# Banded attention and a two-layer MLP on one core: the second layer's 512-token blocks as Strassen's seven products

## The chip, the cores and the metric

The kernel runs on one core of a Trainium2 chip. The core has five engines, each with its own instruction queue: TensorE (PE in the profile; its weight loads are shown apart as PEld), VectorE (DVE), ScalarE (ACT), GpSimd (POOL) and SyncE (SP), which here only issues DMAs. TensorE writes its results to PSUM, eight banks of 512 float32 columns on 128 partitions; the other engines bring them from there to SBUF. The metric is the device time of one execution in microseconds (us); lower is better.

## The reference

Inputs are q, k and v of shape 8 x 8 x 576 x 64 (batch, heads, tokens, head width), the two weight matrices and two scalars s and b. All are float32.

```
scores = q k^T / 8, kept where |i - j| <= 32
attn   = softmax(scores);  x = attn v            # back to 4608 tokens x 512
h      = x w_in                                  # 512 -> 2048
g      = s * relu(h)^2 + b
out    = g w_out                                 # 2048 -> 512, float32
```

The kernel takes bfloat16 operands and accumulates in float32. It multiplies by s and adds the row b * (column sums of w_out) after the second layer, so the second layer itself multiplies relu(h)^2 by w_out.

## The kernel before

**The planner.** The kernel describes its work as tasks: each has a stream (an engine's queue), a list of instructions, an assumed cost, what it reads and writes, and a key, which is a due time. `_Graph.plan` (lines 114 to 220) takes, again and again, the task that could start earliest by its model of costs and DMAs, and the one with the smallest key among equals. This gives each engine a fixed order of instructions. `_Graph.emit` (lines 222 to 311) turns the dependences into semaphore waits. On the chip an engine keeps to its order: an instruction that waits holds all that stands behind it on that engine. Buffers are rings, and a task that writes a slot waits for the last reader of what was there.

**Token blocks.** The 4608 tokens are cut into twelve blocks (`TBLK`, lines 328 to 336): block 0 to 3 of 96, 128, 128 and 160 tokens, and block 4 to 11 of 512 tokens each.

**Attention** (lines 507 to 922) goes through eight batches in units of 128 tokens. For batches 0 and 1, q and k are loaded in pairs of heads, cast into a slot of `NAT` (`turn_pair`, line 575), and turned on TensorE. From batch 2 on, `piece` (line 604) loads three pieces a batch (512 rows of q, 512 rows of k, the last 64 rows of both), casts each into a pair of `NAT` slots on GpSimd and VectorE (line 624), turns it with a DMA that transposes (line 631, on SP's queue; keys go to `KTR`), and reorders the keys on GpSimd into `KT` (line 641). V is loaded to `VST` and cast into `VB` (line 562). A unit's scores (line 675) go through an exponential on ScalarE (line 703) and a mask on VectorE (line 707); then come the product with V (line 733), a reciprocal and a multiplication on VectorE (lines 755 and 757; the result is a slot of `XN`), and a transpose into `XT`: on TensorE and ScalarE for the first three batches, by a DMA on SP's queue (line 781) from then on. The loads of a later batch wait for the products with V of an earlier unit (`paced`, line 532).

**First layer** (`s1`, line 937): for each block and each of the sixteen 128-wide slices of the hidden layer, four matmuls (line 948, one per 128 input columns) into one of two PSUM banks `W`, a Relu on ScalarE into one of three `R1` tiles (line 955), and a square on VectorE into `GT` (line 957). `GT` has two halves of 512 tokens, used in turn.

**Second layer** (`s2`, line 961): for each 128 tokens, sixteen matmuls (line 966) with 128 tokens of `GT` as the weights and 512 columns of `WOUT_BF` moving, in four groups of four, each group needing four slices of `GT`. They gather in one of two banks `O`. `put` (line 979) multiplies by s and adds the row with b on VectorE (line 982) and stores 128 x 512 float32 from SP's queue (line 986). A block of 512 tokens has sixteen groups. The very last 128 tokens are done as two halves of 256 columns. Blocks 0 to 3 go another way (`early`, line 989): their second layer is taken two slices at a time as the output weights arrive.

**The order.** The keys of the two layers (lines 416 to 426) put the second layer of a block beside the first layer of the next one, spread evenly. The attention's keys (`due`, line 444) ask for a unit 14 us and more ahead of its block.

**The rest.** `flag` (line 1044) checks at the end that the exponential sums were in range; if not, a slow general kernel (`general`, line 1066) computes all again, using the weights in SBUF. It doesn't run with these inputs.

Of the kernel before, what the change touches and what calls it, by code (L numbers as in the profile page):

```python
# [313 lines left out]
def bass_sliding_window_symmetric__then__act_starrelu_kernel(  # L314
# [23 lines left out]
    with ExitStack() as es:  # L338
# [19 lines left out]
        NSTG, NNAT, NEX, NXN, NR1, NOUT, XR = 8, 6, 5, 5, 3, 5, 2048  # L358
# [7 lines left out]
        KTR = [sb((128, 4, NPAIR, 144), BF16, "ktr") for _ in range(2)]  # L366
# [3 lines left out]
        KT = [sb((128, NPAIR, S), BF16, "kt") for _ in range(2)]  # L370
        VST = sb((128, NUNIT, H, D), F32, "vst")
        VB = sb((128, 2 * NUNIT, H, VW), BF16, "vb")
# [45 lines left out]
        for m in range(NM + 1):  # L418
            n2 = 4 * len(subs(m - 1)) if m > 0 else 0
            long = (16 * c1(m) if m < NM else 0.0) + n2 * 0.864  # L420
            for ft in range(16):
                P1[m, ft] = at + ft / 16.0 * long
            for i in range(n2):
                P2[4 * subs(m - 1)[0] + i] = at + (i + 0.5) / n2 * long
            at += long
            PH.append(at)
# [70 lines left out]
        for i in range(2):  # L497
            for c0 in (0, WIN + S):
                zero("dve", QT[i][:, :, c0:c0 + WIN], ("QTZ", i, c0), 150, key=-98 if i == 0 else -20)
            add("dve", lambda e, i=i: e.memset(VB[:, i * NUNIT:i * NUNIT + NUNIT, :, :].rearrange("p t h c -> p (t h) c")[:, :, D:D + 1], 1.0), 150,  # L500
# [58 lines left out]
        def cast_v(c, u, key, eng, slack):  # L559
            vs, vb, n = number(c, u) % NUNIT, number(c, u) % (2 * NUNIT), 64 * len(tiles(c, u))  # L560
# [43 lines left out]
        def piece(b, parts, key, waits):  # L604
# [23 lines left out]
            for name, t0, n, p0 in parts:  # L628
                np_, s0, xs = n // 4, t0 // 4, pieces(t0, t0 + n, 64)
                dst = q_later(b)[:, :, :, 16 + s0:16 + s0 + np_] if name == "q" else KTR[slot][:, :, :, s0:s0 + np_]  # L630
# [3 lines left out]
                    writes=[("QT", slot, x, pr) for x in xs for pr in range(NPAIR)] if name == "q" else [("KTR", slot, t0)],  # L634
# [4 lines left out]
                for c in range(t0, t0 + n, 128):  # L639
# [3 lines left out]
                        KTR[slot][:, :, :, c // 4:(c + w) // 4].rearrange("p i a s -> p a s i")),  # L643
                        100 + 5.5 * w, reads=[("KTR", slot, t0)],
# [70 lines left out]
        def av_part(b, u):  # L715
# [3 lines left out]
            vb = number(b, u) % (2 * NUNIT)  # L719
# [4 lines left out]
            def put(h, x, g):  # L724
# [3 lines left out]
                if not 0 <= j < seq_tiles(b):  # L728
# [7 lines left out]
                    rhs=VB[64 * g:64 * g + 64, (vb + j // 2 - u) % (2 * NUNIT), h, 0:D + 1], start=first, stop=True,  # L736
# [6 lines left out]
            reads += [("V", (vb - x) % (2 * NUNIT)) for x in (0, 1) if (x == 0 or u > 0) and (x or tiles(b, u))]  # L743
# [181 lines left out]
        count = {"w": 0, "o": 0, "outs": 0}  # L925
# [11 lines left out]
        def s1(m, f0):  # L937
# [4 lines left out]
            rb = count["w"] % NR1  # L942
# [4 lines left out]
            rt = R1[rb][:, 0:ng * nt].rearrange("p (g c) -> p g c", g=ng)  # L947
# [8 lines left out]
                190 + 0.833 * ng * nt, reads=[("W", wb)], writes=[("R1", rb)], key=key)  # L956
            add("dve", lambda e: e.tensor_tensor(GT[gs][:, f0:f0 + ng, g0:g0 + nt], rt, rt, ALU.mult),  # L957
                130 + 0.53 * ng * nt, reads=[("R1", rb)],
                writes=[r for g in range(ng) for r in gt_res(gs, f0 + g, g0, nt)], key=key)

        def s2(sub, qd, c0=0, cn=DM, shift=0.0):
            ob = count["o"] % 2
            r0 = 128 * sub
            gs, g0 = r0 // 512 % 2, r0 % 512
            key = P2[4 * sub + qd] + shift
            add("pe", [lambda e, fc=fc: e.matmul(O[:, ob, 0:cn],  # L966
                                                 lhsT=GT[gs][:, fc, g0:g0 + 128],
# [6 lines left out]
            if qd < 3:  # L974
                return
# [50 lines left out]
        def second(m):  # L1026
            for sub in subs(m):
                for qd in range(4):
                    s2(sub, qd)
# [256 lines left out]
```

## Time and profile before

| what | value |
|---|---|
| median of 3 timed runs | 321.4 us (320.65 to 321.5) |
| span of the profiled execution, first to last instruction | 319.3 us |
| TensorE busy, granted clock | 301.8 us, 0.995 |
| VectorE busy | 194.1 us |
| ScalarE busy | 138.7 us |
| GpSimd busy | 89.3 us |
| first-layer matmuls of 512 columns | 512, 127.1 us |
| second-layer matmuls of 512 columns | 496, 122.2 us |
| second-layer matmuls of 256 columns | 32, 3.7 us |

The profiler took one execution, whose time is its span; the timed runs were made without it. Busy times of matmuls contain overlap, since one starts before the last has drained: what a matmul costs in a stream is read from the distance between starts. A line of a group gives the code line, the engine, the operation, output and input, shapes and count, then busy time, mean length in ns, and the idle time of the engine in front of them with what ended it. A line of the order in time begins with the start and the length in us. In the chain of waits, SPq is SP's queue and "issue" is time in which an engine waited for nothing that the profile shows.

### The profile page before, as it was taken

The page shows a single profiled execution, that of the slowest core. Times are in us where ns is not written, and L with a number is a line of the kernel's source. Part 1 is how long each engine was busy: PE and PEld are TensorE (multiplying, and loading weights), DVE is VectorE, ACT ScalarE, POOL GpSimd, SP SyncE. Part 2 cuts the span into 40 slices and gives each one's busy share as a digit, 9 for nine tenths or more (in the row PEclk, how much of TensorE's full clock was granted, in tenths as well). Part 3 has the DMA queues.
Part 4 walks back from the last instruction along what each step waited for, and adds up shares of the span by engine and source line. Part 5 has one row for each costly group of instructions (what it writes and reads, how often), then busy time and mean ns, then how long its engine had stood idle before and what let it go on. Part 6 is the DMA issues. An engine that isn't in the chain of part 4 may idle for free.

```text
span 319.3 us, 8165 instructions
## 1 busy us (share of the span) xinstructions
PE 301.8 (95%) x3453; PEld 156.6 (49%) x3453; DVE 194.1 (61%) x378; ACT 138.7 (43%) x214; POOL 89.3 (28%) x102
## 2 busy tenths in 40 slices
PE   3689899999999999988999999999999999999996
PEld 2569764544454444433454444444444444444444
DVE  3777686588777983748576856877545553332412
ACT  3646436346635751444246426544444423333200
POOL 4256764626136134213322160326000000000000
PEclk9999999999999999997999999999999999999999
DMA  7989999988998978799789979999211210000022
GB/s 234 289 248 394 386 319 266 197 161 236 266 191 212 284 128 161 163 310 158 156 225 268 187 154 283 207 170 214 72 50 53 67 60 33 35 35 33 34 83 86
DMA packets 101640, 56.74 MB, mean 178 GB/s; under 512 B 76704, under 2 KB 90784, under 8 KB 101600
## 3 DMA queue, kind: packets, MB, share of 16 engines
q1 hardware_dynamic: 101600, 56.18, 73.6%
q8 instruction: 28, 0.46, 0.7%
q14 instruction: 12, 0.10, 0.1%
HBM read 36.70 MB, written 9.44 MB: 144 GB/s over the span
## 4 chain that ended last, share of the span: by engine, by line
PE 64%; DMA 18%; SPq 9%; DVE 4%; ACT 1%; issue 1%; POOL 1%; POOLq 0%
PE w L948 28%; PE o L966 26%; DMA stg<-in_k_dram 6%; DMA vst<-in_v_dram 5%; SPq L631 4%; DMA stg<-in_q_dram 3%; DMA stg<-in_moe_w_out_dram 3%; PE avn L733 2%; PE avn L1000 2%; PE o L1000 2%; SPq L781 2%; DVE gt L957 1%; SPq L616 1%; PE sc L995 1%; PE sc L675 1%
## 5 line engine op out<-in xcount | busy, mean ns | idle before, releaser
L948 PE MATMUL w<-xt,win 128*128 128x512 bf16 (+3 forms) x768 | 144.0, 329 | 0.8 <-ACT xt L772 0.7
L955 ACT ACTIVATE r<-w 128x512 bf16<-128x512 f32 (+2 forms) x148 | 86.6, 586 | 105.7 <-PE w L948 85.9
L966 PE MATMUL o<-wout,gt 128*128 128x512 bf16 (+1 forms) x528 | 125.7, 374 | 0.1
L957 DVE TENSOR_TENSOR gt<-r 128x512 bf16<-128x512 bf16 (+2 forms) x148 | 77.6, 533 | 70.5 <-ACT r L955 69.9
L948 PEld LDWEIGHTS w<-xt,win 128*128 128x128 bf16 x768 | 63.6, 99 | 59.1 <-issue 1.1
L966 PEld LDWEIGHTS o<-wout,gt 128*128 128x128 bf16 x528 | 50.7, 98 | 57.8 <-DVE gt L957 1.1
L624 POOL CAST nat<-stg 128x1024 bf16<-128x1024 f32 (+1 forms) x21 | 26.6, 1265 | 62.9 <-DMA stg<-in_q_dram 46.3
L641 POOL COPY kt<-ktr 128x512 bf16<-128x512 bf16 (+1 forms) x30 | 31.5, 1049 | 42.2 <-DMA ktr<-nat 40.7
L703 ACT ACTIVATE ex<-sc 128x1024 bf16<-128x1024 f32 (+1 forms) x29 | 29.6, 1022 | 31.3 <-PE avn L733 28.8
L982 DVE SCALAR_TENSOR_TENSOR outs<-o,sb,cvec 128x512 f32<-128x512 f32 (+1 forms) x35 | 25.5, 731 | 15.6 <-PE o L966 15.3
L707 DVE TENSOR_TENSOR ex<-ex,mask 128x1024 bf16<-128x1024 bf16 (+1 forms) x29 | 21.9, 754 | 0.9 <-ACT ex L703 0.3
L733 PE MATMUL avn<-vb,ex 64*64 64x65 bf16 x920 | 19.5, 199 | 3.0 <-DVE ex L707 2.8
L757 DVE TENSOR_TENSOR xn<-avn,rec 128x512 bf16<-128x512 f32 (+1 forms) x30 | 20.7, 689 | 0.9
L733 PEld LDWEIGHTS avn<-vb,ex 64*64 64x64 bf16 x920 | 12.7, 108 | 16.3 <-issue 9.1
L624 DVE CAST nat<-stg 128x1024 bf16<-128x1024 f32 (+1 forms) x15 | 12.4, 829 | 7.4 <-DMA stg<-in_q_dram 5.0
L586 PE MATMUL w<-ident,nat 64*64 64x64 bf16 x288 | 8.8, 217 | 6.7 <-ACT nat L579 4.4
L562 DVE CAST vb<-vst 128x512 bf16<-128x512 f32 (+1 forms) x30 | 13.1, 443 | 1.6 <-DMA vst<-in_v_dram 1.6
L586 PEld LDWEIGHTS w<-ident,nat 64*64 64x64 bf16 x288 | 7.4, 130 | 9.0 <-ACT nat L579 4.4
L675 PE MATMUL sc<-qt,kt 64*64 64x128 bf16 x440 | 11.8, 216 | 0.0
L528 POOL CAST win<-stg 128x1024 bf16<-128x1024 f32 x8 | 8.6, 1074 | 9.0 <-DMA stg<-in_moe_w_in_dram 9.0
L755 DVE RECIPROCAL rec<-avn 128x8 f32<-128x8 f32 (+1 forms) x30 | 6.0, 200 | 8.2 <-PE avn L733 8.2
L829 DVE TENSOR_TENSOR ex<-ex,mask 128x1024 bf16<-128x1024 bf16 (+3 forms) x11 | 7.4, 683 | 4.2 <-ACT ex L826 4.1
(75 smaller groups left out, 139.2 us busy)
## 6 DMA issues: line engine op xcount, KB each, us to landing
out_dram<-outs SPq DMA_DIRECT2D x35, 256.0 KB, 3.2
vst<-in_v_dram SPq DMA_DIRECT2D x32, 256.0 KB, 5.7
stg<-in_q_dram SPq DMA_DIRECT2D x6, 1024.0 KB, 6.9
stg<-in_k_dram SPq DMA_DIRECT2D x6, 1024.0 KB, 11.3
stg<-in_moe_w_in_dram SPq DMA_DIRECT2D x8, 512.0 KB, 7.8
stg<-in_moe_w_out_dram SPq DMA_DIRECT2D x8, 512.0 KB, 9.7
stg<-in_q_dram SPq DMA_DIRECT2D x8, 288.0 KB, 6.0
stg<-in_k_dram SPq DMA_DIRECT2D x8, 288.0 KB, 6.0
```

Of the source, the lines that this page charges most:

```text
L586: add("pe", [lambda e, i=i, p0=p0: e.transpose(view[p0:p0 + 64, i, :], nat[p0:p0 + 64, i * 64:i * 64 + 64], IDENT[p0:p0 + 64, p0:p0 + 64]) ...
L624: add(eng, lambda e, x=x: e.tensor_copy(nat[0:top, 1024 * x:1024 * x + 1024].rearrange("p (i h d) -> p h i d", h=H, i=2), stg[0:top, :].re ...
L641: add("pool", lambda e, c=c, w=w: e.tensor_copy(KT[slot][:, :, c:c + w].rearrange("p a (s i) -> p a s i", i=4), KTR[slot][:, :, :, c // 4: ...
L703: add("act", lambda e, dst=flat_dst, src=flat_src: e.activation(dst, src, AF.Exp, bias=0.0, scale=0.125), 190 + 0.833 * 512 * len(hs), rea ...
L707: add("dve", lambda e, flat=flat, mask=mask: e.tensor_tensor(flat, flat, mask, ALU.mult), 130 + 0.53 * 512 * len(hs), reads=[("E", ei, hp, ...
L733: return [lambda e: e.matmul(av[64 * x:64 * x + 64, h, 0:D + 1], lhsT=buf[64 * g:64 * g + 64, h % 2, h // 2, c:c + 64], rhs=VB[64 * g:64 * ...
L757: add("dve", lambda e: e.tensor_tensor(XN[xi][0:p1, :].rearrange("p (a c) -> p a c", a=H), av[0:p1, :, 0:D], REC[ri][0:p1, :].rearrange("p ...
L948: add("pe", [lambda e, g=g, kc=kc: e.matmul(wt[:, g, :], lhsT=WIN_BF[:, kc, (f0 + g) * 128:(f0 + g + 1) * 128], rhs=XT[:, kc, t0 % XR:t0 % ...
L955: add("act", lambda e: e.activation(rt, wt, AF.Relu, bias=0.0, scale=1.0), 190 + 0.833 * ng * nt, reads=[("W", wb)], writes=[("R1", rb)], ...
L957: add("dve", lambda e: e.tensor_tensor(GT[gs][:, f0:f0 + ng, g0:g0 + nt], rt, rt, ALU.mult), 130 + 0.53 * ng * nt, reads=[("R1", rb)], wri ...
L966: add("pe", [lambda e, fc=fc: e.matmul(O[:, ob, 0:cn], lhsT=GT[gs][:, fc, g0:g0 + 128], rhs=WOUT_BF[:, fc, c0:c0 + cn], start=(fc == 0), s ...
L982: add("dve", lambda e: e.scalar_tensor_tensor(OUTS[us][:, 0:cn], bank, SB128[:, 0:1], CVEC[:, c0:c0 + cn], ALU.mult, ALU.add), 200 + 1.07 ...
```

## The change

The second layer of the blocks of 512 tokens (blocks 4 to 11) is split two by two by two: the tokens into halves of 256 (t), the hidden slices into even and odd ones (y), the output columns into halves of 256. Instead of eight products of quarter size there are seven, by the Winograd form of Strassen's scheme. Each product is 2 x 8 matmuls of 256 columns: two groups of 128 tokens (j), which share a bank of `O`, and eight slices.

The seven products need sums of the operands. Those of the weights are made once, on GpSimd (`weight_sums`, four subtractions of 128 x 2048; the third overwrites a quarter of `WOUT_BF`). Those of the hidden values are made for each block on VectorE (`total`, four of 128 x 2048, three of them in place in `GT`, one in a new tile `GSUM`). The results are combined in two ways: some products gather in PSUM onto the bank of an earlier product (no `start`), and each is then added on VectorE to an output tile (`combine`, seven a block of 128 x 512). Stores are 256 rows x 256 columns, four a block. In the last block each group j has its bank (`O` and `SC`) and its own combine and store.

The square covers two slices at once in the blocks of 512 tokens: `R1` tiles are 1024 wide, two Relus fill one, and one VectorE instruction squares both.

`NAT` has 4 slots instead of 6, `XN` 4 instead of 5, output tiles 4 instead of 5, `VB` 8 instead of 10, `KTR` one buffer instead of two, and `XT` holds 1536 tokens instead of 2048. The attention's tasks are created up to 896 tokens past a block's end (`XR - 640`), instead of 1024. The general kernel loads its output weights again, as `WOUT_BF` is changed.

```diff
-        NSTG, NNAT, NEX, NXN, NR1, NOUT, XR = 8, 6, 5, 5, 3, 5, 2048
+        NSTG, NNAT, NEX, NXN, NR1, NOUT, NVB, XR = 8, 4, 5, 4, 3, 4, 8, 1536
+        HN, HT = DM // 2, 256
...
-        R1 = [sb((128, 512), BF16, "r1") for _ in range(NR1)]
+        R1 = [sb((128, 1024), BF16, "r1") for _ in range(NR1)]
+        TW = [sb((128, 8, HN), BF16, "tw") for _ in range(3)]
+        GSUM = sb((128, 8, HT), BF16, "gsum")
...
+            both = ng == 1
+            half = f0 % 2 if both else 0
+            rb = count["r"] % NR1
+            count["r"] += half if both else 1
...
+            if both and not half:
                 return
-            count["o"] += 1
-            put(sub, ("O", ob), O[:, ob, 0:cn], c0, cn, key)
+            f1, nf = (f0 - 1, 2) if both else (f0, ng)
+            rr = R1[rb][:, 0:nf * nt].rearrange("p (g c) -> p g c", g=nf)
+            add("dve", lambda e: e.tensor_tensor(GT[gs][:, f1:f1 + nf, g0:g0 + nt], rr, rr, ALU.mult),
...
+        def weight_sums():
+            key = P2["b", NE, 0] - 12.0
+            for dst, a, b, reads, writes in ((T1, B12, B11, WOUTS, [("T", 1)]), (T3, B22, B12, WOUTS, [("T", 3)]),
+                                             (B12, B22, T1, [("T", 1)], WOUTS), (T4, B21, B12, WOUTS, [("T", 4)])):
+                add("pool", lambda e, dst=dst, a=a, b=b: e.tensor_tensor(dst, a, b, ALU.subtract), 4600.0,
+                    reads=reads, writes=writes, key=key)
...
+            def product(n, bank, lhs, lres, rhs, rres, first):
+                for j in (0, 1):
...
+                    add("pe", [lambda e, g=g, j=j, dst=dst: e.matmul(dst, lhsT=lhs[:, g, 128 * j:128 * j + 128], rhs=rhs[:, g, :],
+                                                       start=first and g == 0 and (apart or j == 0), stop=(g == 7),
+                                                       skip_group_check=True) for g in range(8)],
...
+            total(GSUM[:], a21, a22, ALU.add, r21 + r22, ["GSUM"], early_key)
+            total(a21, a11, a21, ALU.subtract, r11 + r21, r21, early_key)
+            product(0, 0, a11, r11, B11, WOUTS, True)
+            combine(0, 0, slots[0], True, 0, 0)
+            product(1, 1, a12, r12, B21, WOUTS, True)
+            combine(1, 1, slots[0], False, 0, 0)
+            store(slots[0], 0, 0, key[3])
+            total(a11, GSUM[:], a11, ALU.subtract, ["GSUM"] + r11, r11, key[1])
+            total(a12, a12, a11, ALU.subtract, r11 + r12, r12, key[3])
+            product(2, 0, a11, r11, B12, WOUTS, False)
+            combine(2, 0, slots[1], True, HN, 0)
+            product(3, 1, GSUM[:], ["GSUM"], T1, [("T", 1)], True)
+            combine(3, 1, slots[2], True, HN, 1)
+            product(4, 0, a21, r21, T3, [("T", 3)], False)
+            combine(4, 0, slots[2], False, HN, 1)
+            store(slots[2], HN, 1, key[9])
+            product(5, 1, a12, r12, B22, WOUTS, False)
+            combine(5, 1, slots[1], False, HN, 0)
+            store(slots[1], HN, 0, key[11])
+            product(6, 0, a22, r22, T4, [("T", 4)], False)
+            combine(6, 0, slots[3], True, 0, 1)
+            store(slots[3], 0, 1, key[13])
...
-            while made < min(T, TBLK[m][0] + TBLK[m][1] + 1024):
+            while made < min(T, TBLK[m][0] + TBLK[m][1] + XR - 640):
```

More of the change, by code (lines that the diff above doesn't have):

```diff
@@ L922, in attention @@
             yield T
-        count = {"w": 0, "o": 0, "outs": 0}
+        count = {"w": 0, "r": 0, "outs": 0}
         def place(m):
@@ L1024, in bass_sliding_window_symmetric__then__act_starrelu_kernel @@
             s1(NE, ft)
[L1026 to L1029, printed above, removed]
+        weight_sums()
         for m in range(NE + 1, NM):
@@ L1107, in turned @@
                     writes=[(name, t0 // 128)], key=step())
+            for i in range(8):
+                stg = STG[i % 4].rearrange("p (a c) -> p a c", a=2)
+                add("act", lambda e, i=i, stg=stg: e.dma_start(
+                    stg, moe_w_out.rearrange("(fc p) c -> p fc c", p=128)[:, 2 * i:2 * i + 2, :]), 600.0,
+                    writes=[("in", i % 4)], key=step(), dma=("l", 16, 103.0))
+                add("dve", lambda e, i=i, stg=stg: e.tensor_copy(WOUT_BF[:, 2 * i:2 * i + 2, :], stg), 700,
+                    reads=[("in", i % 4)], writes=["wout"], key=step())
             SS, PP = STG[7][:, 0:512], STG[7][:, 512:1024]
@@ L1174, in layer @@
                                                      start=(fc == 0), stop=(fc == 15)) for fc in range(16)], 3500,
-                    reads=[("g", f0) for f0 in range(0, 16, 4)], writes=["o"], key=step())
+                    reads=["wout"] + [("g", f0) for f0 in range(0, 16, 4)], writes=["o"], key=step())
                 us = t0 // 128 % 2
```

121 lines of the change are left out of this document (74 added, 47 removed).

## The prediction

> **What bounds the kernel now.** I read the page's busy times, then the chain that ended last, TensorE's order in time with its idle gaps, the groups by shape, and busy time by stage.
>
> ```profile
> span 319.3 us, 8165 instructions
> PE 301.8 (95%) x3453; PEld 156.6 (49%) x3453; DVE 194.1 (61%) x378; ACT 138.7 (43%) x214; POOL 89.3 (28%) x102
> PE 64%; DMA 18%; SPq 9%; DVE 4%; ACT 1%; issue 1%; POOL 1%; POOLq 0%
> ```
>
> TensorE (PE) is busy 95% of the span and is 64% of the chain. That doesn't yet say that fewer matmul columns shorten the run: an order may fill a wait for attention with second-layer work. So its order in time (start, length, what, count):
>
> ```profile
> 126.77 3.63 PE L966 MATMUL o<-wout,gt 128*128 128x512 bf16 x16
> 130.33 0.32 PE L733 MATMUL avn<-vb,ex 64*64 64x65 bf16 x16
> 130.48 0.39 PE L675 MATMUL sc<-qt,kt 64*64 64x128 bf16 x16
> 130.72 0.32 PE L733 MATMUL avn<-vb,ex 64*64 64x65 bf16 x16
> 130.98 1.04 PE L966 MATMUL o<-wout,gt 128*128 128x512 bf16 x4
> 131.85 1.89 PE L948 MATMUL w<-xt,win 128*128 128x512 bf16 x8
> ...
> 188.50 2.76 PE L966 MATMUL o<-wout,gt 128*128 128x512 bf16 x12
> 191.19 0.32 PE L733 MATMUL avn<-vb,ex 64*64 64x65 bf16 x16
> 191.35 0.39 PE L675 MATMUL sc<-qt,kt 64*64 64x128 bf16 x16
> 191.59 0.32 PE L733 MATMUL avn<-vb,ex 64*64 64x65 bf16 x16
> 191.84 1.04 PE L966 MATMUL o<-wout,gt 128*128 128x512 bf16 x4
> 192.72 1.46 PE L948 MATMUL w<-xt,win 128*128 128x512 bf16 x6
> ```
>
> Ahead of a block's first layer (L948) stand runs of second-layer groups (L966) with attention between them: filler until that block's attention is there. At 131.85 the filler is used up: second layers of blocks 4 and 5 are complete. At 192.72, where block 8 begins, seven of block 7's sixteen groups are left. From 214 on the two layers alternate one to one, and from 192.7 to 302.0 TensorE is busy for 109.23 of 109.30 us. So up to 192.7 the attention's supply sets when blocks begin; behind it TensorE sets the end.
>
> The supply, in the chain of waits, goes by loads, casts, transposing DMAs and VectorE, and it stops TensorE once for long:
>
> ```profile
> 134.55 7.04 DMA stg<-in_q_dram
> 141.60 0.02 issue
> 141.62 0.69 DVE nat L624
> 142.31 1.17 DVE gt L957
> 143.49 0.13 DVE rec L755
> 143.62 0.02 issue
> 143.64 0.69 DVE xn L757
> 144.33 0.61 DVE ex L707
> 144.94 0.04 issue
> 144.98 0.32 PE avn L733 x16
> ```
>
> One cast that waits for a load holds the squares and the masks queued behind it on VectorE; TensorE idles 2.83 us and the granted clock of 140 to 150 is 0.83.
>
> **The change part by part.**
>
> *Fewer columns.* The price of 256-column matmuls is in the kernel's last rows, by the results that follow each group (start, length):
>
> ```profile
> 309.37 0.75 DVE L982 SCALAR_TENSOR_TENSOR outs<-o,sb,cvec 128x512 f32<-128x512 f32 x1 [2.70 <-PE o L966]
> 312.82 0.75 DVE L982 SCALAR_TENSOR_TENSOR outs<-o,sb,cvec 128x512 f32<-128x512 f32 x1 [2.70 <-PE o L966]
> 314.57 0.48 DVE L982 SCALAR_TENSOR_TENSOR outs<-o,sb,cvec 128x256 f32<-128x256 f32 x1 [1.00 <-PE o L966]
> 316.31 0.48 DVE L982 SCALAR_TENSOR_TENSOR outs<-o,sb,cvec 128x256 f32<-128x256 f32 x1 [1.26 <-PE o L966]
> ```
>
> Sixteen 512-column matmuls take 312.82 - 309.37 = 3.45 us (216 ns), sixteen of 256 take 1.74 (109 ns). A block costs 4 x 3.45 = 13.80 before and 112 x 0.109 = 12.18 after: 1.62 less. The weight load (98 ns) still fits beneath each matmul. Blocks 8 to 11 save 6.48 on TensorE's own path. Blocks 4 to 7 would save as much, but block 8 can't start earlier than its attention; all they can give is that block 7's seven leftover groups are done by then, 7 x 0.864 = 6.05. That fits: TensorE was busy for 123.2 of the 126.7 us from 66 to 192.7, and would need 123.2 + 6.05 - 6.48 = 122.8. Kept: 12.5 us, with 3.9 us of slack before block 8.
>
> *VectorE.* The squares become eight of 1024 a block instead of sixteen of 512. Those average 549 ns from 66 to 192.7 (35.16 us for 64), 8.8 us a block; 128x1024 masks took 0.69 us undisturbed and 0.71 on average, so I take 0.75 with collisions: 6.0. Four sums of 2048 are new: from 0.29 (256) and 0.69 (1024) the slope is 0.52 ns an element, so 1.22 each, 1.34 with the squares' mean collision (0.12); upper end 3.1, from the 512-wide xn row (0.69) at the outs rows' slope (0.75 for 512, 0.48 for 256: 1.05 ns an element, so 2.3) plus one collision of 0.8. I take 1.34, since the squares have the same types and two SBUF operands: 5.4. Combines go from four to seven at 0.745: +2.2. Net +4.8 a block, 19 us over four blocks; VectorE was busy for 90.25 of 126.7 there, so 109, 86%. The cover is its idle time, less of which is left: a late load, as at 134.55, then holds more. Behind 192.7 it has 53 of 109 us free. There I charge 0.8 (0 to 2) for squares or combines that come late.
>
> *Weight sums on GpSimd (POOL).* Four two-input operations of 2048 elements; no such row exists. Bounds: its weight cast at 1.05 us for 1024, so 2.1, and its K reorder at 1.118 for 512, twice for two inputs, so 8.9; I take 4.4, the reorder's rate once, nearest by type. They fall from 42.3 (last output-weight cast) on. Two fill the gaps before the casts of 57.7 to 65.8; the in-place one must wait for the early blocks' reads of the weights (65.6), and with the fourth it stands before the K reorders (72.08) that block 5's attention needs. What queues there slips by 0 to 8 us, by 4 as I take it. In front of block 8 the slack (3.9) covers that: 0 at the end, up to 4. SP's transposes and loads behind them are in order and slip too where they wait for a cast.
>
> The Trainium skill ("GPSIMD Engine Reference", section 3.1) gives 4497 ns for a 2048-element fp32 add; by that estimate the sum is the same.
>
> The sums also meet VectorE. The square at 142.23 took 1.25 us against 0.42 alone, and ended 0.27 after the GpSimd cast of 141.65 to 143.21. As collisions of that size four sums cost 4 x 0.8 = 3.3, within the slack of 3.9: 0. If each stops VectorE for its whole length, 4 x 4.4 = 17.6, of which 13.7 pass the slack; that is a rival below. The Trainium skill ("SBUF — State Buffer", section "SBUF: two separate sides") calls the ports that the two share an exclusive lock, held for the whole instruction; by it the sum would be that rival's. The trace agrees with it for that square; no run shown has so long a GpSimd instruction.
>
> *Buffers.* Four natural-layout slots make a batch's third cast wait for its first transpose: for batch 3 that is 84.96 issued, 6.1 in issue, 4.6 to land at the latest, 95.7, against a cast at 89.5 before and its transposes at 94.23: 0 to 2.9 us, on the batch's last unit, with SP's later transposes and V loads behind. One K buffer: its next writer comes at 91.18, its readers end at 77.6: nothing. V, XN and output slots go round in four units (some 20 us) or a block (28 us) against landings of 3.2 to 5.7: nothing. XT of three blocks: the last piece (256.67) waits for block 8's first layer (done by 214): nothing. With VectorE's load I charge the supply of block 8 with 2.0, between 0 and 8.7 (three batches).
>
> *The end.* Before, second-layer work followed the last first layer at once (301.56). Now block 11's first product needs the last pair of squares (0.60 Relu, 0.70 square, hops: ready 1.4 after), less the block-10 halves left over; then product 2 needs three sums in a row on VectorE (3.7) where products 0 and 1 give 3.5, with combines between. 0.3 to 2.6; I take 1.2. The last combine (0.48) and store are as before. Stores stay four a block (eight small ones in the last, against five).
>
> *Sum.* 12.5 - 2.0 - 0.8 - 1.2 = 8.5: a span of 310.8. The timed median, 321.4, is 2.1 above the profiled span, for what lies around it: 312.9, so **313.0 us**, between 309.2 (12.2 kept) and 317.4 (4.0).
>
> **The rivals.**
>
> *The supply slips, gain mostly gone.* Three batches each 2.9 later give 8.7 and leave 12.5 - 8.7 - 2.0 = 1.8: 319.6. For it: the chain from 76 to 145 is all supply, DMA engines 0.95 busy. Against: the third cast is for the last unit.
>
> *VectorE becomes the bound from 66 to 192.7: slower.* At 3.1 us a sum it needs 90.25 + 4 x (12.4 + 2.2 - 2.8) = 137.5 of 126.7: 10.8 late, and with late combines and the end (2.0 to 4.6) nothing is left; with stops like that of 142 (2.8, and 1.4 of clock), 324. It decides from about 3.0 us a sum. Against: the squares reach two elements a cycle.
>
> *The change doesn't do what it says.* If the load, not the columns, paced 256-column matmuls, at 130 ns a block costs 14.6, 0.8 more: 321.4 + 6.4 + 2.0 = 329.8. Against: the 109 ns.
>
> *The weight sums stop VectorE for their whole length.* 12.5 - 0.8 - 1.2 - 13.7 = -3.2: 324.6 (slower from a stop of 3.6 us each). For it: the square of 142.23. Against: in 42 to 75 much of VectorE's work reads PSUM, and TensorE has first layers that wait for no square.
>
> *Full gain:* no slip, nothing late: 308.9.
>
> **How the numbers follow.** A measurement of this kernel tells about 0.3% (1 us) from no change. Forecast 0.56; full gain 0.06; supply slips 0.16, of which 0.05 ends within 0.3%; VectorE-bound 0.15; weight sums 0.04; loads 0.03. Faster 0.73, same 0.05, slower 0.22. The range, 308 to 324, leaves out some 0.15; the forecast's own is 309.2 to 317.4.
>
> **What would show it.** 112 matmuls of 256 columns a block at 108 to 110 ns; TensorE idle ahead of blocks 5 and 6, little behind 192; sums of 1.2 to 1.4 us; GpSimd sums near 4.4 with VectorE's squares stretched beside them; block 8 begun at 192 to 197. It is wrong if a sum is over 3 us, block 8 starts after 205, or TensorE waits for VectorE over 4 us behind it.

## The result, and the profile after

The changed kernel takes 338.23 us in the median of 4 runs (335.78 to 339.42); the kernel before takes 321.2, now over four runs too (320.65 to 321.5). The ratio is 1.0521, with a 95% interval of 1.0465 to 1.0577: 5.2% slower, where 313.0 was forecast and 324 was the upper end of the range. Here and below, medians are over all runs of a kernel and ratios over its fast runs, those within 1.5% of its fastest.

The lines of the page of the changed kernel that answer to those shown of before: span, busy times, granted clock in 40 slices (in tenths of full speed), chain by engine. The last line is the granted clock of before.

```profile
span 337.7 us, 8823 instructions
PE 301.0 (89%) x3821; PEld 198.2 (59%) x3821; DVE 247.3 (73%) x376; ACT 139.1 (41%) x215; POOL 115.6 (34%) x106
PEclk9999996985899799899999999999999999999999
PE 67%; DVE 14%; DMA 10%; SPq 4%; issue 3%; ACT 1%; POOL 1%; POOLq 0%; DVEq 0%
PEclk9999999999999999997999999999999999999999
```

VectorE's share of the chain has gone from 4% to 14%, and the granted clock has dips in the first half where before there was hardly one: its mean is 0.960 against 0.995.

The operations themselves cost what the prediction said. Groups by shape of the changed kernel (busy time, then mean length in ns; then idle time in front):

```profile
L967 DVE TENSOR_TENSOR gt<-r 128x1024 bf16<-128x1024 bf16 x64 | 49.0, 766 | 28.6 <-ACT r L961 28.1
L1003 DVE TENSOR_TENSOR gt<-gt 128x2048 bf16<-128x2048 bf16 x16 | 22.5, 1408 | 0.0
L1003 DVE TENSOR_TENSOR gsum<-gt 128x2048 bf16<-128x2048 bf16 x8 | 10.9, 1365 | 0.1
L1003 DVE TENSOR_TENSOR gt<-gsum,gt 128x2048 bf16<-128x2048 bf16 x8 | 9.8, 1230 | 0.0
...
L983 POOL TENSOR_TENSOR tw<-wout 128x2048 bf16<-128x2048 bf16 x3 | 12.3, 4113 | 0.2
L983 POOL TENSOR_TENSOR wout<-wout,tw 128x2048 bf16<-128x2048 bf16 x1 | 4.4, 4418 | 4.1 <-PE avn L1089 4.1
```

What they do to others shows in the order in time. Lines of VectorE, GpSimd and TensorE around the four weight sums (L983), with start and length:

```profile
40.98 4.06 POOL L983 TENSOR_TENSOR tw<-wout 128x2048 bf16<-128x2048 bf16 x1
...
41.45 5.61 DVE L967 TENSOR_TENSOR gt<-r 128x512 bf16<-128x512 bf16 x4 [0.35 <-ACT r L961]
...
46.73 4.23 POOL L983 TENSOR_TENSOR tw<-wout 128x2048 bf16<-128x2048 bf16 x1
46.98 4.30 DVE L583 CAST nat<-stg 128x576 bf16<-128x576 f32 x1
...
51.34 0.69 PE L589 MATMUL w<-ident,nat 64*64 64x64 bf16 x18 [4.23 <-DVE nat L583]
...
69.81 4.42 POOL L983 TENSOR_TENSOR wout<-wout,tw 128x2048 bf16<-128x2048 bf16 x1 [4.12 <-PE avn L1089]
...
70.24 1.40 DVE L1071 SCALAR_TENSOR_TENSOR outs<-avn,sb,cvec 128x512 f32<-128x512 f32 x2
...
71.67 3.10 DVE L710 TENSOR_TENSOR ex<-ex,mask 64x1024 bf16<-64x1024 bf16 x1
...
74.83 0.93 PE L736 MATMUL avn<-vb,ex 64*64 64x65 bf16 x24 [2.93 <-DVE ex L710]
...
79.99 4.05 POOL L983 TENSOR_TENSOR tw<-wout 128x2048 bf16<-128x2048 bf16 x1
80.49 6.22 DVE L565 CAST vb<-vst 128x512 bf16<-128x512 f32 x3
...
81.91 2.31 PE L954 MATMUL w<-xt,win 128*128 128x512 bf16 x5 [0.68 <-ACT xt L775]
```

At each of the four, a VectorE instruction begins while the sum runs and ends only when the sum has ended. The cast at 46.98 takes 4.30 us; a cast of this shape took 0.45 in the kernel before (43.42). The mask of 64x1024 at 71.67 takes 3.10, against 0.67 for the same shape with no sum beside it (111.74). TensorE awaits both, idling for 4.23 and 2.93 us. Of the four squares at 41.45 the first alone takes 3.87. Block 4 starts at 81.91 instead of 66.49.

TensorE's waits for VectorE from 66 us to the end (in total, times, longest):

```profile
PE avn L736 <- DVE ex L710: 5.0, 3, 2.9
PE o L1010 <- DVE gt L1003: 4.3, 2, 3.1
PE o L1010 <- DVE gt L967: 3.3, 3, 2.1
```

I split the difference of the spans, 18.4 us, in two ways. By place: block 8 starts at 204.78 instead of 192.72, 12.1 late, and from there to the end it is 132.9 us instead of 126.6, 6.3 more. Of the lateness, 15.4 is there already at block 4; the stretch from block 4 to block 8 gives 3.3 back, but leaves more of the second layer undone: 104 of block 7's 112 matmuls (11.3 us at 109 ns) instead of seven groups (6.05 us).

By kind: I took the distance from each matmul's start to the next and compared it with the matmul's columns at full speed. What is left over counts as a wait if it is over 0.15 us and, for matmuls of 512 columns, over 1.15 times the matmul itself; smaller excesses count as slow matmuls, since a granted clock of 0.50 (shown further below) doubles the distance. Against the kernel before, in us of one profiled execution each:

| kernel | columns | waits | slow matmuls | all |
|---|---|---|---|---|
| the change | -12.8 | +22.2 | +8.2 | +17.8 |
| weight sums in eighths | -12.8 | +17.0 | +4.4 | +8.8 |
| no hidden sums | -12.8 | +7.7 | -0.2 | -5.2 |
| eight quarter products | +1.1 | +3.7 | -1.7 | +3.3 |
| seven from block 8 on | -6.4 | +2.1 | -1.8 | -6.0 |
| seven in blocks 8 to 10 | -4.8 | +0.7 | +1.8 | -2.1 |
| seven from block 8 on, sums on GpSimd | -6.4 | +8.0 | +0.5 | +2.2 |

The first row says it: the columns are saved, to within 0.2 us of the 8 x 1.62 forecast, and the waits that come with them are 1.7 times as large. (The other rows are the experiments below. Profiled executions scatter by one or two us against the medians, so the verdicts go by the timed ratios. The last column is the distance from first to last matmul, and differs by a few tenths from the sum of the others.)

Up to the start of block 4 the same measure gives 10.0 us more of waits and 4.6 more of slow matmuls than before: nearly all of the 15.4. Of these waits 7.2 us are the two that end at the cast and at the mask held beneath a sum, and from 38 us on none ends at a GpSimd instruction. The granted clock was 0.50 from 49.3 to 56.1 and from 73.2 to 86.9, each time from within one of the two waits on.

### The profile page after: what moved, and what is told of

It reads as the page before. It is cut to its first block, busy times and chain, and to the rows that moved or that the text cites. A ratio compares the mean times of both kernels' runs of the same rounds, so it can differ in the third digit from the quotient of the medians.

```text
span 337.7 us, 8823 instructions
## 1 busy us (share of the span) xinstructions
PE 301.0 (89%) x3821; PEld 198.2 (59%) x3821; DVE 247.3 (73%) x376; ACT 139.1 (41%) x215; POOL 115.6 (34%) x106
## 4 chain that ended last, share of the span: by engine, by line
PE 67%; DVE 14%; DMA 10%; SPq 4%; issue 3%; ACT 1%; POOL 1%; POOLq 0%; DVEq 0%
PE w L954 32%; PE o L1010 21%; DMA stg<-in_k_dram 3%; DVE gt L967 3%; PE avn L736 3%; DMA stg<-in_moe_w_in_dram 2%; PE o L1089 2%; PE avn L1089 2%; DVE ex L710 2%; DMA qt<-nat 2%; DVE gt L1003 2%; SPq L634 2%; DVE outs L1026 2%; PE sc L678 1%; DMA vst<-in_v_dram 1%
## 5 line engine op out<-in xcount | busy, mean ns | idle before, releaser
L967 DVE TENSOR_TENSOR gt<-r 128x1024 bf16<-128x1024 bf16 (+3 forms) x84 | 64.4, 775 | 36.5 <-ACT r L961 36.0
L1010 PE MATMUL o<-wout,gt 128*128 128x256 bf16 x480 | 62.6, 280 | 8.6 <-DVE gt L1003 4.3
L1010 PEld LDWEIGHTS o<-wout,gt 128*128 128x128 bf16 x480 | 47.0, 100 | 23.6 <-DVE gt L1003 4.9
L644 POOL COPY kt<-ktr 128x512 bf16<-128x512 bf16 (+1 forms) x30 | 40.1, 1338 | 9.1 <-DMA ktr<-nat 7.6
L1010 PE MATMUL o<-tw,gt 128*128 128x256 bf16 x240 | 31.1, 273 | 0.0
L1010 PEld LDWEIGHTS o<-tw,gt 128*128 128x128 bf16 x240 | 23.3, 98 | 8.3
L1026 DVE SCALAR_TENSOR_TENSOR outs<-o,sb,cvec 128x512 f32<-128x512 f32 (+1 forms) x32 | 22.6, 707 | 5.5 <-PE o L1010 5.2
L1003 DVE TENSOR_TENSOR gt<-gt 128x2048 bf16<-128x2048 bf16 x16 | 22.5, 1408 | 0.0
L1026 DVE SCALAR_TENSOR_TENSOR outs<-o,sb,outs 128x512 f32<-128x512 f32 (+1 forms) x24 | 17.0, 707 | 6.3 <-PE o L1010 6.3
L565 DVE CAST vb<-vst 128x512 bf16<-128x512 f32 (+1 forms) x30 | 19.2, 652 | 1.6 <-DMA vst<-in_v_dram 1.6
## 6 DMA issues: line engine op xcount, KB each, us to landing
stg<-in_k_dram SPq DMA_DIRECT2D x6, 1024.0 KB, 11.3
```

The lines of the kernel that those rows point to most:

```text
L644: add("pool", lambda e, c=c, w=w: e.tensor_copy(KT[slot][:, :, c:c + w].rearrange("p a (s i) -> p a s i", i=4), KTR[:, :, :, c // 4:(c + w ...
L967: add("dve", lambda e: e.tensor_tensor(GT[gs][:, f1:f1 + nf, g0:g0 + nt], rr, rr, ALU.mult), 130 + 0.55 * nf * nt, reads=[("R1", rb, x) fo ...
L1003: add("dve", lambda e: e.tensor_tensor(dst, x, y, op), 1240.0, reads=reads, writes=writes, key=k)
L1010: add("pe", [lambda e, g=g, j=j, dst=dst: e.matmul(dst, lhsT=lhs[:, g, 128 * j:128 * j + 128], rhs=rhs[:, g, :], start=first and g == 0 an ...
L1026: add("dve", lambda e, src=src, dst=dst, other=other: e.scalar_tensor_tensor(dst, src, SB128[:, 0:1], other, ALU.mult, ALU.add), 200 + 1.0 ...
```

## The experiments

The theory after the result: the weight sums on GpSimd block VectorE for as long as they last, in the stretch in which attention is built up, and block 4's lateness is never made up. The rivals: GpSimd's time or a late key reorder rather than the block on VectorE; the smaller buffers; VectorE's new work; the coarser second layer.

**Weight sums left out, and on VectorE.** The first kernel replaces the sums by raw quarters of the weights; the second only moves them to VectorE.

```diff
-        T1, T3, T4 = (t[:] for t in TW)
+        T1, T3, T4 = B12, B22, B21
...
-        weight_sums()
+        g.writer.update({("T", i): g.writer[("Wout", 3, 1)] for i in (1, 3, 4)})
```

> The weight sums are left out (products read unsummed quarters of the output weights, so blocks 4 to 11 of the output are not the reference's); all matmuls, hidden sums and combines stay. Theory A (the four GpSimd instructions hold VectorE and the casts from 41 to 84 us, block 4 starts 15.4 us late, and nothing later takes that up): 15 to 18 less than 338.2, so 320 to 323, block 4 started near 66. Theory B (the loss comes from the hidden sums, the combines and the smaller buffers; an early delay is taken up by later waits): 330 to 338.

```diff
-                add("pool", lambda e, dst=dst, a=a, b=b: e.tensor_tensor(dst, a, b, ALU.subtract), 4600.0,
+                add("dve", lambda e, dst=dst, a=a, b=b: e.tensor_tensor(dst, a, b, ALU.subtract), 1240.0,
```

> The same four weight sums on VectorE, output as the reference's. Theory A: about 1.22 us each, no long GpSimd instruction, so 5 us of VectorE instead of 15 to 18 of delay: 322 to 328. Theory B: 333 to 340, since VectorE gets still more.

Measured: 322.23 us, ratio to before 1.0046 [1.0005, 1.0088], without the sums; 322.65 us, 1.0051 [1.0024, 1.0078], with the sums on VectorE. Both take away some 15 us (1.0521 less 1.0046 or 1.0051, of 321 us), and they are equal within the intervals. So the four additions cost about 15 us on GpSimd (13 to 17 by the intervals) and about nothing on VectorE. Block 4 starts at 67.0 and 68.0 us in their profiled runs, near the 66.49 of before, as the first theory expected. But both kernels are still 1.5 us slower than before, where the forecast without any cost of the sums was 8.5 us faster.

**The same sums in eighths, still on GpSimd.**

```diff
-                add("pool", lambda e, dst=dst, a=a, b=b: e.tensor_tensor(dst, a, b, ALU.subtract), 4600.0,
-                    reads=reads, writes=writes, key=key)
+                for h in range(8):
+                    add("pool", lambda e, dst=dst, a=a, b=b, h=h: e.tensor_tensor(dst[:, h:h + 1, :], a[:, h:h + 1, :], b[:, h:h + 1, :], ALU.subtract), 650.0,
+                        reads=reads, writes=writes, key=key)
```

> Each GpSimd weight sum cut into eight of 256 elements, the same work and place. If the length of one instruction is what hurts (VectorE waits for the whole of it): each wait at most 0.7 us, more than half of the delay gone, 323 to 330. If GpSimd's time hurts (17 us of its queue ahead of casts and reorders): 335 to 342, as there are more fixed costs.

Measured: 330.76 us, 1.0314 [1.0254, 1.0375], between the two expectations and just above the first. Its group of sums into the new tiles (the fourth, in place, is in the order in time below):

```profile
L984 POOL TENSOR_TENSOR tw<-wout 128x256 bf16<-128x256 bf16 x24 | 19.0, 791 | 1.9
```

The order in time at block 4's start and at TensorE's longest wait behind it, lines of GpSimd and TensorE:

```profile
67.38 1.04 PE L954 MATMUL w<-xt,win 128*128 128x512 bf16 x4 [0.68 <-ACT xt L775]
...
68.10 6.12 POOL L984 TENSOR_TENSOR wout<-wout,tw 128x256 bf16<-128x256 bf16 x7
74.28 2.47 POOL L627 CAST nat<-stg 48x1024 bf16<-48x1024 f32 x2
76.84 0.72 POOL L984 TENSOR_TENSOR wout<-wout,tw 128x256 bf16<-128x256 bf16 x1
77.64 1.00 POOL L984 TENSOR_TENSOR tw<-wout 128x256 bf16<-128x256 bf16 x1
78.69 4.80 POOL L644 COPY kt<-ktr 128x512 bf16<-128x512 bf16 x4
79.86 0.64 PE L678 MATMUL sc<-qt,kt 64*64 64x128 bf16 x16 [4.48 <-POOL kt L644]
```

GpSimd spends more time on the sums than when they were whole (19.0 and, for the eighths in place, 6.8 us, 25.8 against 16.7), and yet the kernel is 6.6 us faster (0.0207 of 321; 4 to 9 by the intervals). What shrank is the longest time for which one instruction can hold VectorE: block 4 starts at 67.38, so the lateness that the whole sums bring about there is gone. What is left arises further on. Block 5 starts at 108.09 instead of 98.53, and of that 4.48 us is TensorE's wait for a key reorder on GpSimd, which stood behind the last eighths on GpSimd's own queue. In the changed kernel TensorE's waits for a key reorder come to 1.3 us in all from 66 us on. So the rival on GpSimd's time is right for the sums in eighths, and the trace doesn't show it in the 15 us of the whole ones.

**Sums on GpSimd, but later.** The place is tried below, behind the kernels that use seven products only from block 8 on.

**The smaller buffers alone, and the wide squares alone,** each as a change to the kernel before.

```diff
-        NSTG, NNAT, NEX, NXN, NR1, NOUT, XR = 8, 6, 5, 5, 3, 5, 2048
+        NSTG, NNAT, NEX, NXN, NR1, NOUT, NVB, XR = 8, 4, 5, 4, 3, 4, 8, 1536
...
```

> The kernel before with the change's smaller buffers alone (NAT 4, XN 4, output tiles 4, VB 8, one KTR, XT of 1536 tokens, attention 896 tokens ahead). Theory A: within 1.5 us of 321.2. Theory C (the supply of attention slips with the buffers, up to 2.9 us a batch): 324 to 330.

```diff
-        R1 = [sb((128, 512), BF16, "r1") for _ in range(NR1)]
+        R1 = [sb((128, 1024), BF16, "r1") for _ in range(NR1)]
...
+            if both and not half:
+                return
...
```

> The kernel before with squares over two slices alone (XN and output tiles at 4 for room). Theories D and F both: 319.5 to 321.5; half as many two-input instructions can meet GpSimd's, which is worth up to 1 us.

Measured: 320.46 us, 1.0002 [0.9965, 1.0038], with the buffers; 323.7 us, 1.0028 [0.9982, 1.0074], with the wide squares. That median is above the range expected; the ratio answers to about 322, just above the range's upper end. Neither is told from no change. The buffers by themselves drop out as a cause, and with them their part of the 2.0 us that I charged for the supply; whether they cost something together with the sums was not tried.

**What is left: the sums of hidden values, and the quarter products.** To the kernel with the weight sums on VectorE, the first edit leaves out the four totals of a block (product 3 then uses `a22`). The second makes eight plain quarter products of a block, with no sums at all and four combines.

```diff
             def total(dst, x, y, op, reads, writes, k):
-                add("dve", lambda e: e.tensor_tensor(dst, x, y, op), 1240.0, reads=reads, writes=writes, key=k)
+                return
```

> Weight sums on VectorE as in the run before, but the four hidden sums of each block are left out (products read unsummed halves, so blocks 4 to 11 of the output are not the reference's): 40 us less of VectorE, no chain from the squares over the sums to the products; matmuls, combines, squares and buffers stay. Theory D (VectorE's sums and the waits on them eat the columns' gain): 310 to 315 against 322.7. Theory F (a product needs a whole block's slices, so nothing of a block's own second layer can fill waits any more, and the supply of attention sets when blocks begin): 318 to 322.

```diff
...
+            quarters = ((0, 0, a11, r11, a12, r12, B11, B21), (HN, 0, a11, r11, a12, r12, B12, B22),
+                        (HN, 1, a21, r21, a22, r22, B12, B22), (0, 1, a21, r21, a22, r22, B11, B21))
+            for i, (c0, t, x, rx, y, ry, bx, by) in enumerate(quarters):
+                product(2 * i, i % 2, x, rx, bx, WOUTS, True)
+                product(2 * i + 1, i % 2, y, ry, by, WOUTS, False)
+                combine(2 * i + 1, i % 2, slots[i], True, c0, t)
+                store(slots[i], c0, t, key[4 * i + 3])
...
```

> The same halves, 256-column matmuls, wide squares and buffers, but the eight plain quarter products, two gathered in PSUM each, with four combines a block; no weight sums, no hidden sums. TensorE has the old columns. Theory F: the coarse dependence alone costs: 323 to 328. Theory D: 320 to 322, as only the sums and combines hurt. The end should cost about 1 us less than the change's.

Measured: 318.42 us, 0.9934 [0.9890, 0.9979], without the totals; 325.23 us, 1.0134 [1.0075, 1.0194], with eight quarter products. The first lies in the range of theory F and outside that of D, the second in that of F. The totals, with the waits on them, cost 0.0117 of 321, 3.8 us: the difference of 1.0051 and 0.9934 (2 to 5 us by the intervals). And the quarter products by themselves, with the columns of before, cost 4.3 us, of which 1.1 is the price of two matmuls of 256 columns against one of 512 (the table). TensorE's waits from 66 us on in that kernel:

```profile
PE o L1010 <- DVE gt L967: 2.6, 3, 1.6
PE avn L767 <- DVE xn L760: 1.9, 1, 1.9
PE avn L736 <- POOL kt L644: 1.2, 1, 1.2
```

A 512-column group needed four of a block's slices. A quarter product needs eight, every second one, so none can begin until the block's first layer is nearly done, and there is less to fill TensorE's waits for attention with; that this is the whole of the 4.3 us is argued, not shown. Such a wait for the last squares is the first line; before, TensorE hadn't one that the view lists.

**Seven products only where TensorE sets the end.** Blocks 4 to 7 go back to the second layer of the kernel before; the weight sums are on VectorE, behind the first squares of block 8.

```diff
+        SEVEN = (8, 9, 10, 11)
...
         def second(m):
+            if m in SEVEN:
+                seven(m)
+                return
...
+            for sub in rest if m == NM - 1 else subs(m):
+                for qd in range(4):
+                    s2(sub, qd)
...
```

> Seven products in blocks 8 to 11 alone, where TensorE sets the end; blocks 4 to 7 by the old second layer; weight sums on VectorE after block 8's first squares; output as the reference's. If the gain of blocks 4 to 7 can't be had and that of 8 to 11 can: 4 x 1.62 = 6.5 less, 2.0 back at the end: 315.5 to 318. If stalls follow the seven products wherever they are: 319 to 323.

Measured: 318.36 us, 0.9939 [0.9900, 0.9979]: 2.0 us faster than before, 0.4 above the range expected. Seven products in blocks 4 to 7 as well (the kernel with the sums on VectorE, 1.0051) make it 0.0112 or 3.6 us slower (2 to 5 by the intervals), where they should have kept 6.05. The end of this kernel, lines of TensorE's order in time:

```profile
294.99 1.04 PE L1045 MATMUL o<-tw,gt 128*128 128x256 bf16 x8
296.57 1.05 PE L1045 MATMUL sc<-wout,gt 128*128 128x256 bf16 x8 [0.54 <-DVE gt L968]
...
299.20 1.04 PE L1045 MATMUL sc<-wout,gt 128*128 128x256 bf16 x8
301.42 1.05 PE L1045 MATMUL o<-wout,gt 128*128 128x256 bf16 x8 [1.18 <-DVE gt L1038]
```

Groups of eight follow each other at 0.87 us when nothing is awaited. From 294.99 to 296.57 it is 1.58, and in front of 301.42 another 1.35 is lost (299.20 + 0.87 = 300.07): 2.1 us, since nothing is left to run while the last squares and three totals are made. So next the last block was taken out.

**Three blocks, and four that end before the last.** Seven products in blocks 8 to 10; before block 11, one addition on VectorE restores the quarter of the weights (its lines stand in the kernel above already, and are reached now). Then the same with block 7 taken in.

```diff
-        SEVEN = (8, 9, 10, 11)
+        SEVEN = (8, 9, 10)
...
             if m == NM - 1:
                 add("dve", lambda e: e.tensor_tensor(B12, T1, B11, ALU.add), 1240.0, reads=[("T", 1)], writes=WOUTS, key=P2[4 * rest[0]] - 1.0)
```

> The kernel with seven products from block 8 on, except that block 11, the last, goes back to the second layer of the kernel before; VectorE restores the changed quarter of the weights (T1 + B11) in one addition of about 1.2 us ahead of it. Theory (the saving of columns is kept where TensorE sets the end, and the end itself pays about 2 us for sums and staged halves): against the run with seven products in blocks 8 to 11 (318.4 us) the columns of one block, 1.6 us, are given back and the 2.1 us that TensorE lost behind the last first-layer tile are not; the time is 317.5 to 318.5, that is 2.5 to 4 us below the kernel before. Rival (the end costs nothing beyond what the kernel before pays too): only the 1.6 us are given back and the time is 319.5 to 320.5.

> The kernel with seven products in blocks 8, 9 and 10, with block 7 taken in as well (seven products in blocks 7 to 10, the weight sums on VectorE now behind the first squares of block 7). Theory (TensorE sets the end from the start of block 8, and in that kernel three quarters of block 7's second layer lie behind this start): another 1.2 to 1.6 us is kept, and the time is 316 to 317 where the three blocks took 317.9. Rival (the four weight sums and block 7's hidden sums, some 10 us more of VectorE's time, now lie where attention still supplies block 8): block 8 starts 2 to 5 us later and the time is 318.5 to 321.5.

Measured: 317.89 us, 0.9906 [0.9870, 0.9941], with three blocks; 317.08 us, 0.9868 [0.9822, 0.9915], with blocks 7 to 10. The three blocks come out where the theory had them, 3.0 us below before, and TensorE's order shows that nothing is lost behind the last first-layer tile: 80 matmuls in one run. By the timed runs alone they can't be told from the four blocks (0.9906 and 0.9939, overlapping): the columns given back and the waits saved are nearly equal.

```profile
299.20 1.04 PE L1045 MATMUL o<-tw,gt 128*128 128x256 bf16 x8
300.07 14.18 PE L1001 MATMUL o<-wout,gt 128*128 128x512 bf16 x80
```

Block 7 does no harm, against the rival; whether it gains its 1.2 to 1.6 us can't be told from the overlapping intervals. This kernel, 1.3% faster than before (0.9 to 1.8), has the lowest time of all that leave nothing out.

**The late place for the sums on GpSimd.** The kernel with seven products from block 8 on, its weight sums back on GpSimd.

> The kernel with seven products from block 8 on, its four weight sums moved from VectorE to GpSimd, still behind the first squares of block 8. It leaves nothing out. Theory (each GpSimd sum holds VectorE's two-input operations for as long as it lasts): four times about 4.2 us in which squares stand still in block 8, where VectorE is busy for some 21 of 28 us; it comes 10 to 17 us late, TensorE waits for squares or sums in block 8 or 9, and the time is 5 to 15 us above the run with the sums on VectorE, 323 to 333. Rival (the sums only did harm because they lay in the supply of blocks 4 to 7, where attention sets the end): here little waits for VectorE, and the time is within 2 us of the sums on VectorE, 317 to 320.5.

Measured: 324.03 us, 1.0130 [1.0047, 1.0213]. The same four instructions cost 0.0191 of 321, 6.1 us, against the sums on VectorE (3 to 9 by the intervals). The order in time around two of them:

```profile
220.35 4.37 POOL L985 TENSOR_TENSOR wout<-wout,tw 128x2048 bf16<-128x2048 bf16 x1
220.74 4.53 DVE L711 TENSOR_TENSOR ex<-ex,mask 128x1024 bf16<-128x1024 bf16 x1
...
225.19 5.03 DVE L566 CAST vb<-vst 128x512 bf16<-128x512 f32 x2
...
225.32 0.43 PE L737 MATMUL avn<-vb,ex 64*64 64x65 bf16 x16 [5.37 <-DVE ex L711]
...
225.83 4.12 POOL L985 TENSOR_TENSOR tw<-wout 128x2048 bf16<-128x2048 bf16 x1
...
226.33 5.84 PE L1045 MATMUL o<-wout,gt 128*128 128x256 bf16 x32
```

A mask that takes 0.68 (231.92 in the same trace) takes 4.53 beneath the sum, TensorE idles 5.37 for it, and the 32 matmuls that follow take 5.84 us, where 32 at 109 ns are 3.5: the granted clock was 0.50 from 224.0 to 230.8. So it isn't the place alone: VectorE is held at either place, and the place decides between 6 and 15 us. The theory's range of 5 to 15 us holds, at its low end; what TensorE waited for was a mask, though, and not a square.

## Why the prediction was wrong

Between the 313.0 forecast and the 338.2 measured lie 25.2 us. The weight sums account for 15.1 (1.0521 less 1.0051), and the columns of blocks 4 to 7 for 9.7 (6.05 forecast as gained, 3.6 lost). The other terms nearly cancel. Both of these failed, and no rival joined the two, so the measured time lies above all of them.

*Weight sums on GpSimd: the step that failed most.* Its size was right: 4.1 to 4.4 us an operation, against 4.4. What failed is "as collisions of that size four sums cost 4 x 0.8 = 3.3, within the slack of 3.9: 0". The collision isn't of the size of a 1.2 us square but lasts to the end of the GpSimd instruction: 4.30 us for a cast, 3.10 for a mask, 3.87 for a square. That was the rival with 0.04 of the chance. It had the mechanism, and 324.6 for it; its argument against, that much of VectorE's work from 42 to 75 reads PSUM, fell with the cast and the mask above, which read SBUF. Measured, the sums cost about 15 us, where that rival had 13.7 past the slack. Up to block 4, 4.6 us of it are slow matmuls at a granted clock of 0.50, for which the sum had no term.

The rule of the Trainium skill ("SBUF — State Buffer", section "SBUF: two separate sides"), an exclusive lock held for the whole instruction, is what these rows show: 4.30 us for the cast beneath a sum of 4.23. The prediction named the rule and the square that agreed with it, but gave its rival 0.04; it had no row with a long GpSimd instruction.

*The slack.* It was counted once, at block 8. But the sums' stops fall before block 4, and there the kernel before had filler for TensorE that is used up in the meantime: from 74.83 to 81.91 the changed kernel runs only small attention matmuls between short waits. Nor did the slack of 3.9 show afterwards. From block 4 to block 8 the changed kernel got back 3.3 of 15.4 us only by leaving 5.3 us more of block 7's second layer for later, and by the measure of the table TensorE's waits in that stretch rose from 3.5 to 9.5 us.

*The columns of blocks 4 to 7, "6.05 kept".* This failed too, independently of the sums. At block 8's start the changed kernel has 104 of block 7's 112 matmuls left, 11.3 us, where "block 7's seven leftover groups are done by then" said none and the kernel before had 6.05 us. Seven products in blocks 4 to 7 cost 3.6 us instead of saving 6.05, by the pair of runs with the sums on VectorE. Two parts of it are measured, on the whole kernel and not for these blocks alone: quarter products that wait for all of a block's first layer (4.3 us with no sums), and the totals (3.8). The prediction treated the second layer of these blocks as filler of a given length; it missed that the new filler comes ready later and needs VectorE, which is part of the supply, to be made ready.

Its premise was too strict as well. Block 8 was said not to start before its attention, at 192.72; with the smaller buffers alone it started at 187.06 and in the kernel with seven products from block 8 on at 182.42, in both with twelve of block 7's sixteen groups left instead of seven. So an earlier start and a longer remainder are exchanged for each other, and the start of block 8 alone doesn't measure progress.

*The columns of blocks 8 to 11, 6.48.* Saved as forecast: 0.87 us for eight matmuls of 256. With the sums on VectorE and blocks 4 to 7 as before, 2.0 us of it arrives. TensorE's waits between blocks 8 and 11 came to 4.4 us in the changed kernel against 0.2 before, where 0.8 was charged for squares or combines that come late (the longest three: 1.35 us for a mask, 1.34 for a key reorder, 1.03 for a combine); 2.7 of it lies between blocks 9 and 10, where the run with seven products from block 8 on lost 3.7, mostly in attention that waited 3.5 us for a key reorder on GpSimd.

*The end, 1.2 (0.3 to 2.6).* Right in kind, 2.1 in size, as in the kernel with seven products from block 8 on. The two waits were named in the prediction's order; in the changed kernel:

```profile
320.35 1.05 PE L1010 MATMUL sc<-wout,gt 128*128 128x256 bf16 x8 [0.54 <-DVE gt L967]
...
325.20 1.05 PE L1010 MATMUL o<-wout,gt 128*128 128x256 bf16 x8 [1.18 <-DVE gt L1003]
```

*VectorE's operations.* Right: totals of 1.23 to 1.41 us against 1.34, squares of 0.766 against 0.75, combines of 0.740 against 0.745. So the rival that needs 3.0 us a sum fell. Where the prediction erred is in what that work is worth: 19 us of it were called covered by idle time, and 3.8 us of the totals reached the end.

*Buffers.* 2.0 charged with the supply; by themselves they made no difference that could be measured.

*From the span to the time.* 2.1 us was added; the runs of both kernels show 1.7 (339.42 against a span of 337.7, 321.01 against 319.3). The remaining 0.4 is scatter between runs.

*The granted clock.* It had no term in the sum of the forecast. In the changed kernel the matmuls that follow a long wait run at about half speed, as here after 3.10 us:

```profile
110.54 3.42 PE L1010 MATMUL o<-wout,gt 128*128 128x256 bf16 x16 [3.10 <-DVE gt L1003]
...
114.18 1.91 PE L1010 MATMUL o<-tw,gsum 128*128 128x256 bf16 x16
```

The same sixteen matmuls take 3.42 and, 3.6 us later, 1.91 us. The column "slow matmuls" of the table puts this at 8.2 us for the whole kernel, and in the kernels with 8 us of added waits or less it doesn't stand out from the scatter (-1.8 to +1.8). It comes with the waits, and in the changed kernel adds about a third to their price. The Trainium skill ("TensorE: Matmul & The Clock Gate", "Part 1: The HAM clock gate") states half the clock after an idle window of about 3.4 us, until TensorE has been busy for as long; the two rows agree with the half, after a wait a little shorter than that. The length of the wait alone doesn't decide it: in the sums in eighths the granted clock was 0.52 from 102.0 to 105.5, behind a wait of 2.37 us, and in the kernel with seven products from block 8 on it stayed at 1.00 through and behind a wait of 3.53 (at 215.89).

*What stays open.* How the 9.7 us of blocks 4 to 7 divide between the later start of the quarter products and the totals there; and whether a better order could fill the waits in these blocks. Each edit also lets the planner order the tasks anew, and no experiment holds the order fixed.

## What to carry to other kernels

A long GpSimd instruction must be priced as that much of VectorE's time as well, wherever VectorE's casts and two-input operations are on the path: the same four additions cost 15 us there, 6 us at a quieter place, and nothing that could be measured on VectorE, where they take 1.2 us instead of 4.2. A saving of TensorE's work counts only in the stretch where TensorE sets the end: with the sums on VectorE, the seven products gained 1.3% when used in blocks 7 to 10 and lost 0.5% when used in all eight, since their operands come ready later and must be made by an engine that feeds the others. In the last block, the waits for the products' operands (2.1 us) used up the columns saved (1.6).

## What the runs showed of the hardware that was not expected

- A VectorE cast with one input, 128x576 from float32, was held for 4.30 us by a GpSimd addition of 4.23; so the block isn't confined to VectorE's two-input operations. Two operations that read PSUM were not held: the output rows at 70.24 took 1.40 us together in the middle of the sum of 69.81 to 74.23, and the mask right behind them took 3.10.
- GpSimd's instructions were longer as well: its key reorder of 128x512 took 1.372 us on average in the changed kernel, with VectorE busy for 247.3 us, against 1.118 before, with 194.1. That VectorE's work is the reason isn't shown apart.
- Cutting a GpSimd addition of 2048 elements (4.1 us) into eighths gave 791 ns each, 6.3 us together, and the kernel was 6.6 us faster with it.
